# Top-k attention and two MLP layers: the second product in spare columns of a score bank, the mask from an unnegated threshold

## The chip, the cores and the metric

The kernel runs on one core of a Trainium2 chip. The metric is the device time of one execution, in microseconds (us); lower is better. Every comparison is between executions of whole kernels on the chip.

## The reference

```python
# q, k, v: (4, 8, 576, 64): batch, heads, sequence, head size
scores = scale * np.matmul(q, k.transpose(0, 1, 3, 2))       # scale = 1/8
kth = np.partition(scores, -32, axis=-1)[..., -32:-31]       # the 32nd largest of each row
scores = np.where(scores >= kth, scores, -1000000000.0)
attn = np.exp(scores - np.max(scores, axis=-1, keepdims=True))
attn = attn / (np.sum(attn, axis=-1, keepdims=True) + 1e-09)
x = np.matmul(attn, v)                                       # then laid out as 2304 tokens x 512
# two layers, weights 512 x 2048 and 2048 x 512 each
h = x @ w_in;  g = h * (1 / (1 + np.exp(-1.702 * h)));  x = g @ w_out
h = x @ w_in2; g = P3(h) / (1 + |b0| |h| + |b1| h*h + 1e-6);  out = g @ w_out2
# P3(h) = a0 + a1 h + a2 h*h + a3 h*h*h
```

## The kernel before

The 2304 tokens are cut into 18 tiles of 128. For each tile the attention goes through 8 heads, so there are 144 steps, numbered 0 to 143 and called heads here. The MLP layers work on groups of two tiles (one at the end), in units whose hidden rows fill one 128x512 block.

A head goes through these stations (lines of the kernel before):

- TensorE multiplies q and k into a score tile `S` (line 585), 128 rows by two halves of 288 columns. Each half lies in a PSUM bank of its own with room for 512. There are two `S` tiles, so four banks.
- VectorE finds the 32nd largest score of each row: four times the eight largest (`mx`, line 594), and between them three times those eight are struck out (`W`, line 596). The first pass reads `S`, the others `W`.
- VectorE negates the threshold (line 598). ScalarE subtracts it, and a Prelu with a slope of 2^100 sends what lies below it far down (line 599). With that `S` is read for the last time.
- VectorE makes the bias of the exponential (lines 600 and 601), ScalarE takes the exponential (line 602) and a 16-bit copy (line 604), GpSimd the rest that the copy leaves (line 606).
- A DMA transposes both into `AT` (one tile), and TensorE multiplies `AT` and `V` into a bank `misc` (line 625: 64 columns and one with the row sums).
- VectorE inverts the sums (line 635), and ScalarE scales the 64 columns into `x` (line 636).

The remaining PSUM banks are one for `misc`, which the small sums of line 310 use too, one for the hidden rows `h` of the MLPs (line 748), and two for their outputs `acc` (lines 830 and 833). `NH` and `NMISC` count the first two kinds. The MLPs' elementwise work is on ScalarE (lines 769, 784, 798, 799, 807), GpSimd (773, 809) and VectorE (777).

What each engine does and in which order is settled ahead of the run. Each operation carries a cost and a due time in heads, and a planner (`schedule`) puts it on its engine where it would be ready first. On the chip every engine then goes through its list in order. An operation that waits holds up all behind it on that engine. The due times of the second product and of what follows it come from `LAV`, in heads. `lock` tells the planner whether an operation keeps VectorE and GpSimd apart; it changes no instruction.

Of the kernel before, what the change touches and what calls it, by code (L numbers as in the profile page):

```python
# [19 lines left out]
FAR = 2.0 ** 100  # L20
# [188 lines left out]
def kernel(  # L209
# [69 lines left out]
    def misc():  # L279
        return buf("misc", [P, 512], F32, NMISC, pp)  # L280

# [9 lines left out]
    kc = cp.tile([P, 4], F32, name="kc")  # L291
    POOL.memset(kc[:, 2:3], scale)
    POOL.memset(kc[:, 3:4], -scale)
# [257 lines left out]
    def q_scale(t, hp, prio):  # L551

        qi = QI[t, hp // 2]
        ei = EI[t, hp] = buf("ei", [P, 2], F32, 3)

        def f():
            for r0, n, bb, _ in segs(t):
                r = slice(r0, r0 + n)
                POOL.tensor_scalar(ei[r], kc[r, 2:4], qi[r, 2:3], kinv[r, bb, hp:hp + 1], ALU.mult, ALU.mult)

        op("POOL", 2 * PTINY * len(segs(t)), f, [qi] + [KI[bb, hp] for _, _, bb, _ in segs(t)], [ei], prio)
# [10 lines left out]
    def attend(i, prio):  # L572
        t, h = divmod(i, H)
        qs, ei = QS[t, h // 4], EI[t, h // 2]
# [14 lines left out]
        nm = buf("nm", [P, 2], F32, 3)  # L589
# [25 lines left out]
    def attend_av(i, prio):  # L615
        t, h = divmod(i, H)
        sg = segs(t)
        at = ATS.pop(i)
        ps = misc()

        def av(r0, n, V):
            for j in range(KM + 1):
                kp = P if j < KM else ST + 1
                for x, lo, hi in ((0, D, 2 * D + 1), (0, 0, D), (1, D, 2 * D + 1)):
                    PE.matmul(ps[r0:r0 + n, :hi - lo], at[:kp, x, j, r0:r0 + n], V[:kp, h % 2, j, lo:hi],  # L625
                              start=(j == 0 and lo == D and x == 0), stop=(j == KM and x == 1), skip_group_check=True)

        if h == 0:
            XT[t] = buf("x", [P, DM], F32, NX)
        x = XT[t]  # L630
        for r0, n, bb, _ in sg:
            V = VS[bb, h // 2]
            op("PE", 0.5, lambda r0=r0, n=n, V=V: av(r0, n, V), [at] + [VS[b2, h // 2] for _, _, b2, _ in sg], [ps] + ([x] if h == 0 else []), prio)
# [273 lines left out]
    for t in range(NT):  # L907
        for hq in range(H // 4):
            at(t * H + 4 * hq - QLAG, q_prep, t, hq, t * H + 4 * hq - QLAG)
        for hp in range(H // 2):  # L910
            at(t * H + 2 * hp - 1, q_scale, t, hp, t * H + 2 * hp - 1)
    for i in range(NS):
        at(i, attend, i, i)
        at(i + LAV, attend_av, i, i)
# [3 lines left out]
    for layer, p0 in ((1, W1P), (2, W2P)):  # L918
        for f2 in range(NPAIR):
            at(p0 + f2 * WR, w_load, layer, f2, p0 + f2 * WR)  # L920
    for g, ts in enumerate(grans):
        p = max(first[max(gb[g])] - 3, W1P + NPAIR * WR)
        at(p, x_scale, g, p)
        for t in ts:
            at((t + 1) * H - 0.9 + LAV, x_done, t, (t + 1) * H - 0.9)
# [10 lines left out]
    for n, (layer, g, only) in enumerate(seq):  # L936
        done = only is None or only == len(grans[g]) - 1
        if layer == 1:
            p = max(p, (grans[g][-1 if only is None else only] + 1) * H + LAV + MLAG)
# [44 lines left out]
LAV = 1.5  # L984
NMISC = 1
NH = 1
# [23 lines left out]
FREE = ("t", "misc")  # L1010
# [30 lines left out]
```

## Time and profile before

| what | value |
|---|---|
| time, median of 3 runs | 1317.77 us (1316.63 to 1322.38) |
| the profiled execution's own time | 1319.38 us |
| its span in the profile | 1317.6 us |
| busy TensorE / VectorE / ScalarE / GpSimd | 80% / 82% / 80% / 67% of the span |

The span runs from the first to the last instruction that the profile shows; the execution's time has 1.8 us more around it. Busy shares are averages over stretches with different limits: from 0 to 400 us the weights of the MLPs are prepared beside the first heads, from 400 to 1110 us attention and MLPs run side by side, and behind that only MLP work is left.

### The profile page before, as it was taken

To read this page: it belongs to the slowest core of one execution; us is meant where nothing else is said; L and a number is where in the kernel's file an instruction comes from. 1 tells how busy PE (TensorE), PEld (TensorE's weight loads), DVE (VectorE), ACT (ScalarE), POOL (GpSimd) and SP (SyncE) were. 2 spreads that over 40 slices of the span, in tenths; PEclk is the share of its full clock that TensorE was granted. 3 is DMA by queue.
4 is the path that set the end of the run, shared out by engine and by line. 5 is a ranking of instruction groups with operands and counts; after the bars stand their busy time and mean duration, and the time that the engine had idled before them with its cause. 6 is when DMAs were issued, how large, how long until landed. Compare 5 with 4: busy or idle time off the path is not lost.

```text
span 1317.6 us, 25473 instructions
## 1 busy us (share of the span) xinstructions
PE 1058.3 (80%) x8812; PEld 711.5 (54%) x8812; DVE 1078.3 (82%) x2649; ACT 1050.6 (80%) x1939; POOL 881.1 (67%) x998
## 2 busy tenths in 40 slices
PE   1222474744699899999899999999999999999997
PEld 0111352523466566666656665665666577566664
DVE  4999999999999899999989999999999999202010
ACT  6767675767689988999999898888889889667674
POOL 5576774645556776888676688667767866656554
PEclk9999975875699999999989999999999999999999
DMA  9667789777747984797777469666856963734375
GB/s 268 166 186 199 195 240 261 219 213 144 148 67 155 207 187 81 164 216 161 164 196 189 77 162 207 142 131 160 184 112 142 219 116 83 182 118 147 119 237 187
DMA packets 366145, 222.40 MB, mean 169 GB/s; under 512 B 316608, under 2 KB 328896, under 8 KB 366016
## 3 DMA queue, kind: packets, MB, share of 16 engines
q1 hardware_dynamic: 366016, 220.78, 69.6%
q8 instruction: 69, 1.13, 0.4%
q14 instruction: 60, 0.49, 0.1%
HBM read 136.32 MB, written 13.11 MB: 113 GB/s over the span
## 4 chain that ended last, share of the span: by engine, by line
DVE 45%; PE 22%; ACT 13%; POOL 7%; DMA 6%; issue 6%; SPq 1%; POOLq 0%; ACTq 0%; DVEq 0%
DVE mx L594 15%; DVE W L596 13%; PE h L748 9%; PE acc L830 7%; ACT t L769 5%; DMA AT<-A 5%; PE acc L833 3%; POOL t L773 3%; DVE ring L357 3%; DVE ring L359 3%; DVE t L777 2%; POOL A L606 2%; DVE ring L355 2%; PE misc L625 1%; DVE V L462 1%
## 5 line engine op out<-in xcount | busy, mean ns | idle before, releaser
L773 POOL TENSOR_TENSOR t<-t,t 128x512 f32<-128x512 f32 x288 | 380.4, 1321 | 142.1 <-ACT t L769 72.8
L594 DVE MAX8 mx<-W 128x8 f32<-128x576 f32 x432 | 323.2, 753 | 5.2
L830 PE MATMUL acc<-ring,t 128*128 128x512 f32 x576 | 271.1, 603 | 7.3 <-POOL t L773 4.9
L606 POOL TENSOR_TENSOR A<-E,A 128x576 f16<-128x576 f32 x144 | 189.7, 1318 | 66.3 <-ACT A L604 57.0
L748 PE MATMUL h<-xh,W 128*128 128x128 f16 (+1 forms) x2304 | 214.8, 253 | 15.2 <-ACT t L769 13.4
L596 DVE MATCH_REPLACE8 W<-mx,W 128x576 f32<-128x576 f32 x288 | 213.5, 742 | 0.0
L748 PE MATMUL h<-yh,ring 128*128 128x256 f16 (+1 forms) x1920 | 201.8, 262 | 12.7 <-ACT t L769 12.2
L748 PEld LDWEIGHTS <-W 128*128 128x128 f16 x2304 | 186.6, 102 | 44.4 <-issue 24.0
L748 PEld LDWEIGHTS <-ring 128*128 128x128 f16 x1920 | 171.8, 98 | 57.0 <-issue 37.0
L585 PE MATMUL S<-K,qs 128*128 128x288 f16 (+1 forms) x640 | 118.6, 317 | 79.8 <-ACT E L599 74.6
L833 PE MATMUL acc<-W,gh 128*128 128x512 f16 x576 | 175.4, 387 | 2.4 <-ACT gh L807 2.4
L602 ACT ACTIVATE E<-E,nm,ei 128x576 f32<-128x576 f32 x144 | 124.3, 865 | 44.1 <-DVE nm L601 30.2
L777 DVE SCALAR_TENSOR_TENSOR t<-t,ab,t 128x512 f32<-128x512 f32 x72 | 65.3, 907 | 114.9 <-ACT t L769 114.7
L830 PEld LDWEIGHTS acc<-ring,t 128*128 128x128 f32 x576 | 102.1, 192 | 99.5 <-issue 89.2
L625 PEld LDWEIGHTS <-AT 128*128 128x128 f16 (+2 forms) x2400 | 96.3, 106 | 92.9 <-DMA AT<-A 66.3
L625 PE MATMUL misc<-V,AT 128*128 128x65 f16 (+5 forms) x2400 | 106.6, 202 | 47.6 <-DMA AT<-A 34.1
L599 ACT ACTIVATE E<-S,nm 128x576 f32<-128x576 f32 x144 | 106.4, 739 | 40.4 <-DVE nm L598 32.7
L769 ACT ACTIVATE t<-h,cf 128x512 f32<-128x512 f32 (+1 forms) x160 | 95.8, 638 | 39.9 <-PE h L748 31.2
L585 PEld LDWEIGHTS <-qs 128*128 128x128 f16 (+1 forms) x640 | 65.3, 110 | 111.0 <-issue 86.8
L594 DVE MAX8 mx<-S 128x8 f32<-128x576 f32 x144 | 108.6, 754 | 12.4 <-PE S L585 11.6
L809 POOL TENSOR_TENSOR gl<-t,gh 128x512 f16<-128x512 f32 x72 | 84.4, 1172 | 48.5 <-ACT gh L807 47.4
L833 PE MATMUL acc<-W,gl 128*128 128x512 f16 x288 | 111.2, 386 | 4.9 <-POOL gl L809 4.9
(145 smaller groups left out, 1729.5 us busy)
## 6 DMA issues: line engine op xcount, KB each, us to landing
ring<-scr SPq DMA_DIRECT2D x160, 512.0 KB, 3.9
ring<-in_moe_w_in_dram SPq DMA_DIRECT2D x16, 1024.0 KB, 5.7
ring<-in_moe_w_out_dram SPq DMA_DIRECT2D x16, 1024.0 KB, 6.0
ld<-in_v_dram SPq DMA_DIRECT2D x32, 256.0 KB, 3.4
out_dram<-t SPq DMA_DIRECT2D x18, 256.0 KB, 3.6
ld<-in_k_dram SPq DMA_DIRECT2D x16, 256.0 KB, 3.7
lq<-in_q_dram SPq DMA_DIRECT2D x32, 128.0 KB, 3.2
scr<-ring SPq DMA_DIRECT2D x8, 512.0 KB, 6.8
```

The costliest lines, as they stand in the source:

```text
L585: PE.matmul(s[:n, c, :SH], qs[:, 2 * (h % 4) + x, :n], K[:, h % 2, c * SH:(c + 1) * SH], start=(x == 0), stop=(x == 1))
L594: op("DVE", dve(S, not r), lambda r=r: DVE.max(mx[:, r], w.t if r else sv()), [w if r else s], [mx], prio)
L596: op("DVE", dve(S, not r) + 0.068, lambda r=r: DVE.match_replace(w.t if r else two(w.t), mx[:, r], w.t if r else sv(), NEG), [mx, w if r e ...
L599: op("ACT", act(S, True) + APA, lambda: ACT.activation(two(e.t), sv(), AF.Prelu, bias=nm[:, 0:1], alpha=FAR), [s, nm], [e], prio)
L602: op("ACT", act(S) + 2 * APA, lambda: ACT.activation(e.t, e.t, AF.Exp, bias=nm[:, 1:2], scale=ei[:, 0:1]), [e, nm, ei], [e], prio)
L606: lo = lambda en: en.tensor_tensor(A[:, 1, :S], e.t, A[:, 0, :S], ALU.subtract)
L625: PE.matmul(ps[r0:r0 + n, :hi - lo], at[:kp, x, j, r0:r0 + n], V[:kp, h % 2, j, lo:hi], start=(j == 0 and lo == D and x == 0), stop=(j == ...
L748: PE.matmul(o, w[:, half, kd * 256 + jj * P: kd * 256 + (jj + 1) * P], xy[:, tl, l * ND + kd, :], start=(n == 0), stop=(n == 3 * ND - 1))
L769: op("ACT", act(w, True) + APA, lambda f2=f2, c=c: ACT.activation(dst[:, c], src[:, c], func, bias=bias(f2) if bias else 0.0, scale=sc(f2) ...
L773: op("POOL", pool_tt(512), lambda: POOL.tensor_tensor(o.t, x.t, y.t, f), [x, y], [o], prio, alt=("DVE", dve(512), lambda: DVE.tensor_tenso ...
L830: PE.matmul(acc[j].t, u.gate[:, c], w[:, jj * DM:(jj + 1) * DM], start=st, stop=sp)
L833: PE.matmul(acc[j].t, l[:, c], w[:, half, jj * DM:(jj + 1) * DM], start=(st and n == 0), stop=(sp and n == 2))
```

## The change

```diff
-FAR = 2.0 ** 100
+NEAR = 2.0 ** -90
...
     def misc():
-        return buf("misc", [P, 512], F32, NMISC, pp)
+        return buf("h", [P, 512], F32, NH, pp)
...
 def q_scale(t, hq, prio):          # once per four heads; before, once per two
-                POOL.tensor_scalar(ei[r], kc[r, 2:4], qi[r, 2:3], kinv[r, bb, hp:hp + 1], ALU.mult, ALU.mult)
+                POOL.tensor_scalar(ei[r], kinv[r, bb, 2 * hq:2 * hq + 2], qi[r, 2:3], -scale / NEAR, ALU.mult, ALU.mult)
...
 def attend(i, prio):
+        if i >= LA:
+            av_product(i - LA, s, prio)
...
-        op("DVE", TINY, lambda: DVE.tensor_scalar(nm[:, 0:1], mx[:, 3, 7:8], -1.0, None, ALU.mult), [mx], [nm], prio)
-        op("ACT", act(S, True) + APA, lambda: ACT.activation(two(e.t), sv(), AF.Prelu, bias=nm[:, 0:1], alpha=FAR), [s, nm], [e], prio)
-        op("DVE", 2 * TINY, lambda: (DVE.tensor_scalar(nm[:, 1:2], mx[:, 3, 7:8], mx[:, 0, 0:1], ei[:, 0:1], ALU.subtract, ALU.mult),
-                                     DVE.tensor_scalar(nm[:, 1:2], nm[:, 1:2], EBITS * LN2, None, ALU.add)), [mx, ei], [nm], prio)
-        op("ACT", act(S) + 2 * APA, lambda: ACT.activation(e.t, e.t, AF.Exp, bias=nm[:, 1:2], scale=ei[:, 0:1]), [e, nm, ei], [e], prio)
+        op("ACT", act(S, True) + APA, lambda: ACT.activation(two(e.t), sv(), AF.Prelu, bias=mx[:, 3, 7:8], scale=-1.0, alpha=NEAR), [s, mx], [e], prio)
+        op("POOL", 2 * PTINY, lambda: (POOL.tensor_scalar(nm.t, mx[:, 0, 0:1], mx[:, 3, 7:8], es(), ALU.subtract, ALU.mult),
+                                       POOL.tensor_scalar(nm.t, nm.t, NEAR, EBITS * LN2, ALU.mult, ALU.add)), [mx, ei], [nm], prio, lock=False)
+        op("ACT", act(S) + 2 * APA, lambda: ACT.activation(e.t, e.t, AF.Exp, bias=nm.t, scale=es()), [e, nm, ei], [e], prio)
+        if i >= LA:
+            av_rows(i - LA, s, [e], prio)
...
-    def attend_av(i, prio):
-        ps = misc()
+    def av_product(i, s, prio):
...
-                    PE.matmul(ps[r0:r0 + n, :hi - lo], at[:kp, x, j, r0:r0 + n], V[:kp, h % 2, j, lo:hi],
+                    PE.matmul(s[r0:r0 + n, 0, SH:SH + hi - lo], at[:kp, x, j, r0:r0 + n], V[:kp, h % 2, j, lo:hi],
...
+    def av_rows(i, s, after, prio):
...
-        op("DVE", TINY, lambda: DVE.reciprocal(r.t, ps[:, D:D + 1]), [ps], [r], prio)
-        op("ACT", act(D, True) + APA, lambda: ACT.activation(x[:, h * D:(h + 1) * D], ps[:, :D], AF.Copy, scale=r.t), [ps, r], [x], prio,
-           alt=("DVE", dve(D, True) + APD, lambda: DVE.tensor_scalar(x[:, h * D:(h + 1) * D], ps[:, :D], r.t, None, ALU.mult)))
+        op("DVE", TINY, lambda: DVE.reciprocal(r.t, s[:, 0, SH + D:SH + D + 1]), [s, *after], [r], prio, lock=False)
+        op("DVE", dve(D, True) + APD, lambda: DVE.tensor_scalar(x[:, h * D:(h + 1) * D], s[:, 0, SH:SH + D], r.t, None, ALU.mult), [s, r, *after], [x], prio, lock=False)
...
-LAV = 1.5
-NMISC = 1
-NH = 1
+LA = 3
+NH = 2
```

The second product of head i - 3 is written into columns 288 to 352 of the first bank of the `S` tile of head i, ahead of that head's scores. Its rows are read only after the exponential of head i. The last three heads' second products come behind all scores in `S` tiles of their own. The bank that `misc` had goes to `h`, whose two banks the small sums now share. The Prelu takes the threshold itself as bias with a scale of -1 and a slope of 2^-90, and the scale of the exponential is negative and 2^90 times as large. The bias of the exponential moves from VectorE to GpSimd; the scaling of the 64 columns moves from ScalarE to VectorE.

VectorE's list around head 27, the first head whose scores it begins here (tile numbers behind the names; `r` is the inverted row sum of an earlier head). Before:

```order
L594 MAX mx_2676<-S_2655 128x8
L596 MATCH_REPLACE W_2679<-mx_2676,S_2655 128x576
L594 MAX mx_2700<-S_2671 128x8
L594 MAX mx_2676<-W_2679 128x8
L635 RECIPROCAL r_2708<-misc_2681 128x1
L596 MATCH_REPLACE W_2710<-mx_2700,S_2671 128x576
L596 MATCH_REPLACE W_2679<-mx_2676,W_2679 128x576
L594 MAX mx_2700<-W_2710 128x8
L594 MAX mx_2676<-W_2679 128x8
```

Of the change:

```order
L595 MAX mx_2763<-S_2739 128x8
L597 MATCH_REPLACE W_2772<-mx_2763,S_2739 128x576
L595 MAX mx_2763<-W_2772 128x8
L641 RECIPROCAL r_2777<-S_2695 128x1
L597 MATCH_REPLACE W_2772<-mx_2763,W_2772 128x576
L642 TENSOR_SCALAR x_2097<-S_2695,r_2777 128x64
L595 MAX mx_2763<-W_2772 128x8
L597 MATCH_REPLACE W_2772<-mx_2763,W_2772 128x576
L595 MAX mx_2763<-W_2772 128x8
```

Before, two heads (26 and 27) take turns, so that few rows stand directly behind the row of the same head whose result they use. Now head 27 stands alone, and the rows of line 641 and 642 are those of head 23, out of the `S` tile of head 26.

TensorE's list at head 86 (its scores, and the second product of head 83 out of `AT`; `h` and `acc` are MLP work). Before:

```order
L748 MATMUL h_8570<-xh_7408,W_82 128x256
L585 LDWEIGHTS qs_7888
L585 MATMUL S_8603<-K_7547,qs_7888 128x288
...
L625 LDWEIGHTS AT_8551
L625 MATMUL misc_8610<-V_6811,AT_8551 128x65
...
L830 MATMUL acc_1275_8016<-ring,t_8549 128x512
```

Of the change:

```order
L840 MATMUL acc_1184_7813<-ring,t_8177 128x512
L627 LDWEIGHTS AT_8326
L627 MATMUL S_8376<-V_6588,AT_8326 128x65
...
L586 LDWEIGHTS qs_7856
L586 MATMUL S_8376<-K_7331,qs_7856 128x288
...
L758 MATMUL h_8411<-xh_7409,W_80 128x256
```

The second product now stands ahead of the scores, in their tile, and both wait until that tile's earlier head has given up its rows.

## Rows read from the trace of the kernel before

**Rows 1.** The page, part 1: busy us (share of the span) and instructions of each engine.

```profile
PE 1058.3 (80%) x8812; PEld 711.5 (54%) x8812; DVE 1078.3 (82%) x2649; ACT 1050.6 (80%) x1939; POOL 881.1 (67%) x998
```

**Rows 2.** Windows by stage: us, busy of PE, PEld, DVE, ACT, POOL; clock, DMA.

```profile
0.00:400.00 400.00, 190.27 (x1691) 134.07 (x1692) 372.98 (x921) 278.87 (x527) 237.75 (x313) 0.84 0.74 192
400.00:1110.00 710.00, 673.82 (x5629) 451.71 (x5628) 664.06 (x1643) 632.85 (x1161) 524.47 (x582) 1.00 0.73 158
1110.00:1317.60 207.60, 194.24 (x1496) 125.75 (x1493) 41.29 (x87) 138.87 (x254) 118.88 (x104) 1.00 0.53 162
```

**Rows 3.** Windows of line 594 alone: four such instructions are one head.

```profile
0.00:400.00 400.00, 125.65 (x173) 0.84 0.74 192
400.00:1110.00 710.00, 295.44 (x396) 1.00 0.73 158
```

**Rows 4.** Waits from 400 to 1110 us: us in total, times, longest us.

```profile
ACT E L602 <- DVE nm L601: 21.7, 32, 2.0
...
PE misc L625 <- DMA AT<-A: 12.5, 17, 1.8
PE h L748 <- ACT t L769: 12.3, 15, 3.4
DVE r L635 <- PE misc L625: 11.8, 15, 3.8
...
DVE mx L594 <- PE S L585: 8.7, 16, 1.4
...
PE S L585 <- ACT E L599: 3.5, 4, 1.6
```

**Rows 5.** Groups by line and shape: busy us, mean ns of one.

```profile
L636 ACT ACTIVATE x<-misc,r 128x64 f32<-128x64 f32 x144 | 44.6, 310 | 31.3 <-DVE r L635 30.1 <-DVE nm L598 0.4
L559 POOL TENSOR_SCALAR ei<-kc,qi,kinv 128x2 f32<-128x2 f32 x64 | 30.3, 474 | 28.2 <-ACT E L602 27.2 <-POOL V L473 0.2
```

**Rows 6.** VectorE's timeline from 700 to 712 us: start, duration, instruction.

```profile
700.82 0.26 DVE L600 TENSOR_SCALAR nm<-mx,ei 128x1 f32<-128x1 f32 x1
701.11 0.15 DVE L601 TENSOR_SCALAR nm<-nm 128x1 f32<-128x1 f32 x1
701.19 0.08 DVE L596 MATCH_VALUE_LOAD W<-mx,W 128x8 f32 x1
...
702.03 0.76 DVE L594 MAX8 mx<-W 128x8 f32<-128x576 f32 x1
702.83 0.09 DVE L596 MATCH_VALUE_LOAD W<-mx,W 128x8 f32 x1
...
704.48 0.15 DVE L598 TENSOR_SCALAR nm<-mx 128x1 f32<-128x1 f32 x1
704.55 0.16 DVE L635 RECIPROCAL r<-misc 128x1 f32<-128x1 f32 x1
704.62 0.74 DVE L594 MAX8 mx<-S 128x8 f32<-128x576 f32 x1
705.28 0.79 DVE L777 SCALAR_TENSOR_TENSOR t<-t,ab,t 128x512 f32<-128x512 f32 x1
706.00 0.08 DVE L596 MATCH_VALUE_LOAD W<-mx,S 128x8 f32 x1
```

**Rows 7.** VectorE's timeline at 280 us.

```profile
280.02 0.75 DVE L594 MAX8 mx<-S 128x8 f32<-128x576 f32 x1
280.69 0.74 DVE L594 MAX8 mx<-W 128x8 f32<-128x576 f32 x1
```

**Rows 8.** Timeline of ScalarE and TensorE from 700 to 712 us.

```profile
700.06 0.73 ACT L599 ACTIVATE E<-S,nm 128x576 f32<-128x576 f32 x1
...
701.36 0.87 ACT L602 ACTIVATE E<-E,nm,ei 128x576 f32<-128x576 f32 x1
...
702.84 0.62 PE L625 MATMUL misc<-V,AT 128*128 128x65 f16 x15
...
703.30 0.65 PE L585 MATMUL S<-K,qs 128*128 128x288 f16 x4
```

More of the change, by code (lines that the diff above doesn't have):

```diff
@@ L290 @@
     b0, b1 = ab[:, 4:5], ab[:, 5:6]
-    kc = cp.tile([P, 4], F32, name="kc")
-    POOL.memset(kc[:, 2:3], scale)
-    POOL.memset(kc[:, 3:4], -scale)
+    kc = cp.tile([P, 1], F32, name="kc")
     POOL.memset(kc[:, 0:1], 1.0 + 1e-6)
@@ L549, in q_prep, with q_scale @@
         op("SP", 1.3, lambda: SP.dma_start_transpose(qs.t, qh.t.rearrange("p h x n -> p (h x n)")), [qh], [qs], prio, nbytes=P * DM * 5)
-    def q_scale(t, hp, prio):
-        qi = QI[t, hp // 2]
-        ei = EI[t, hp] = buf("ei", [P, 2], F32, 3)
+    def q_scale(t, hq, prio):
+        qi = QI[t, hq]
+        ei = EI[t, hq] = buf("ei", [P, 2], F32, 3)
         def f():
@@ L558, in f @@
                 r = slice(r0, r0 + n)
-                POOL.tensor_scalar(ei[r], kc[r, 2:4], qi[r, 2:3], kinv[r, bb, hp:hp + 1], ALU.mult, ALU.mult)
-        op("POOL", 2 * PTINY * len(segs(t)), f, [qi] + [KI[bb, hp] for _, _, bb, _ in segs(t)], [ei], prio)
+                POOL.tensor_scalar(ei[r], kinv[r, bb, 2 * hq:2 * hq + 2], qi[r, 2:3], -scale / NEAR, ALU.mult, ALU.mult)
+        op("POOL", PTINY * len(segs(t)), f, [qi] + [KI[bb, 2 * hq + x] for _, _, bb, _ in segs(t) for x in range(2)], [ei], prio)
     atiles = [cp.tile([P, 2, (KM + 1) * P], F16, name=f"A{j}") for j in range(NA)]
@@ L573, in attend @@
         t, h = divmod(i, H)
-        qs, ei = QS[t, h // 4], EI[t, h // 2]
+        qs, ei = QS[t, h // 4], EI[t, h // 4]
+        es = lambda: ei[:, h % 4 // 2:h % 4 // 2 + 1]
         sg = segs(t)
@@ L588, in attend @@
         mx = buf("mx", [P, 4, 8], F32, 3)
-        nm = buf("nm", [P, 2], F32, 3)
+        nm = buf("nm", [P, 1], F32, 3)
         w = buf("W", [P, S], F32, 2)
@@ L613 @@
     ATS = {}
-    def attend_av(i, prio):
+    def av_product(i, s, prio):
         t, h = divmod(i, H)
         sg = segs(t)
-        at = ATS.pop(i)
-        ps = misc()
+        at = ATS[i]
         def av(r0, n, V):
@@ L624, in av @@
                 for x, lo, hi in ((0, D, 2 * D + 1), (0, 0, D), (1, D, 2 * D + 1)):
-                    PE.matmul(ps[r0:r0 + n, :hi - lo], at[:kp, x, j, r0:r0 + n], V[:kp, h % 2, j, lo:hi],
+                    PE.matmul(s[r0:r0 + n, 0, SH:SH + hi - lo], at[:kp, x, j, r0:r0 + n], V[:kp, h % 2, j, lo:hi],
                               start=(j == 0 and lo == D and x == 0), stop=(j == KM and x == 1), skip_group_check=True)
+        for r0, n, bb, _ in sg:
+            V = VS[bb, h // 2]
+            op("PE", 0.5, lambda r0=r0, n=n, V=V: av(r0, n, V), [at] + [VS[b2, h // 2] for _, _, b2, _ in sg], [s], prio - 1)
+    def av_rows(i, s, after, prio):
+        t, h = divmod(i, H)
+        ATS.pop(i)
         if h == 0:
@@ L630, in attend_av @@
         x = XT[t]
-        for r0, n, bb, _ in sg:
-            V = VS[bb, h // 2]
-            op("PE", 0.5, lambda r0=r0, n=n, V=V: av(r0, n, V), [at] + [VS[b2, h // 2] for _, _, b2, _ in sg], [ps] + ([x] if h == 0 else []), prio)
         r = buf("r", [P, 1], F32, 3)
-        op("DVE", TINY, lambda: DVE.reciprocal(r.t, ps[:, D:D + 1]), [ps], [r], prio)
-        op("ACT", act(D, True) + APA, lambda: ACT.activation(x[:, h * D:(h + 1) * D], ps[:, :D], AF.Copy, scale=r.t), [ps, r], [x], prio,
-           alt=("DVE", dve(D, True) + APD, lambda: DVE.tensor_scalar(x[:, h * D:(h + 1) * D], ps[:, :D], r.t, None, ALU.mult)))
+        op("DVE", TINY, lambda: DVE.reciprocal(r.t, s[:, 0, SH + D:SH + D + 1]), [s, *after], [r], prio, lock=False)
+        op("DVE", dve(D, True) + APD, lambda: DVE.tensor_scalar(x[:, h * D:(h + 1) * D], s[:, 0, SH:SH + D], r.t, None, ALU.mult), [s, r, *after], [x], prio, lock=False)
+    def attend_av(i, prio):
+        s = buf("S", [P, 2, 512], F32, 2, pp)
+        av_product(i, s, prio)
+        av_rows(i, s, (), prio)
     grans, t = [], 0
@@ L909 @@
             at(t * H + 4 * hq - QLAG, q_prep, t, hq, t * H + 4 * hq - QLAG)
-        for hp in range(H // 2):
-            at(t * H + 2 * hp - 1, q_scale, t, hp, t * H + 2 * hp - 1)
+            at(t * H + 4 * hq - 1, q_scale, t, hq, t * H + 4 * hq - 1)
     for i in range(NS):
         at(i, attend, i, i)
-        at(i + LAV, attend_av, i, i)
     for layer in (1, 2):
@@ L920 @@
             at(p0 + f2 * WR, w_load, layer, f2, p0 + f2 * WR)
+    for i in range(NS - LA, NS):
+        at(NS + 0.1 * (i - NS + LA), attend_av, i, i)
     for g, ts in enumerate(grans):
@@ L924 @@
         for t in ts:
-            at((t + 1) * H - 0.9 + LAV, x_done, t, (t + 1) * H - 0.9)
+            at((t + 1) * H - 0.9 + LA, x_done, t, (t + 1) * H - 0.9)
     def first_layer(g):
@@ L938 @@
         if layer == 1:
-            p = max(p, (grans[g][-1 if only is None else only] + 1) * H + LAV + MLAG)
+            p = max(p, (grans[g][-1 if only is None else only] + 1) * H + LA + MLAG)
         for u in make_units(layer, g, only):
@@ L1009 @@
 PHASES = (16.0, 48.0, 130.0)
-FREE = ("t", "misc")
+FREE = ("t", "h")
 _INS = ['q', 'k', 'v', 'moe_w_in', 'moe_w_out', 'moe2_w_in', 'moe2_w_out', 'moe2_a', 'moe2_b']
```

## Prediction

> **What bounds the kernel now.** I read the stages first. Until 400 us VectorE is busy for 373 of 400 us and TensorE for 190 [rows 2]; 173 instructions of line 594 fall there, so some 43 heads, and 396, some 99 heads, up to 1110 us [rows 3]. In the second stage TensorE is busy for 674 of 710 us and VectorE for 664. Behind it VectorE has 41 us left, and TensorE is busy for 194 of 208 us. So the first stage is VectorE's, the last TensorE's, and in the middle both are nearly full. The page's 80% to 82% for three engines [rows 1] says nothing of this.
>
> Then the waits of the middle stage [rows 4]. TensorE's missing 36 us are mostly waits for the transposed `AT` (12.5 us), for ScalarE to empty the one bank `h` (12.3) and for `S` (3.5). VectorE waits 11.8 us for the second product, ahead of the inversion of its sums, and 8.7 us for scores.
>
> Last, VectorE's own spacing, since its rows overlap. From the start of one search for the largest to the start of the next, of another head, 0.67 us pass [rows 7]. Where the next instruction needs the first one's result it is 0.80 (702.03 to 702.83) [rows 6]: a dependent neighbour costs 0.13 us more, and anything that stands between the two fills that gap.
>
> **The change, part by part.**
>
> *VectorE, taken away.* By start-to-start times, line 600 holds the engine for 0.29 us, line 601 for 0.08, line 598 for 0.07 [rows 6], together 0.44 us a head; their durations add up to more (0.26 + 0.15 + 0.15), but overlap.
>
> *VectorE, added.* One scaling of 128x64 out of PSUM a head. No row shows it on this engine. From below: the inversion of one column holds it for 0.07 us (704.55 to 704.62). From above: the 512 columns of line 777 hold it for 0.72 (705.28 to 706.00) [rows 6], and ScalarE's own row for the same work lasts 0.31 [rows 5]. A line through 0.07 for 1 and 0.72 for 512 columns gives 0.15 for 64, which I take. By the section on the TRN2 errata of the Trainium skill's page "VectorE: DVE Perf Modes" such an operation out of PSUM takes 120 cycles and one for each element, an estimate of 0.19 us, which would make the first stage 1.6 us worse; no run here shows it yet.
>
> *VectorE, moved.* The order shows a loss. Of the six places in a head where a search and a strike-out of one head can stand directly behind each other, 14 in all do so in heads 0 to 43 before, and 89 after the change: the two heads that took turns now mostly come one after the other, because a score tile is given back later. In heads 44 to 143 it is 268 before and 244 after.
>
> So for heads 0 to 43, where VectorE sets the pace: 43 x 0.44 = 18.9 us less, 40 x 0.15 = 6.0 us more, (89 - 14) x 0.13 = 9.8 us more. That is 3 us gained. The bounds of the scaling make it 6 us gained (0.07) or 3 us lost (0.31). For the rest: 101 x 0.44 = 44 us less, and 28 places where line 598 stood directly behind its search, 3.6 us less; 104 x 0.15 = 15.6 us more; 24 x 0.13 = 3.1 us less. That is 35 us less for VectorE.
>
> On the gaps the Trainium skill's page "VectorE: DVE Perf Modes", section "The DRAIN you can't avoid", disagrees: it says that eight chained copies took the same time with a semaphore behind each and with one at the end, so that only the count matters. The trace's 0.80 against 0.67 speaks against that here. By the rule the first stage would gain 12.9 us in place of 3, and the whole would end 10 us lower.
>
> *TensorE, middle stage.* Its work stays the same: the same matrix products in other banks, and by the order almost the same MLP work between the same heads. With VectorE 35 us shorter, TensorE is the bound of this stage, and it can win back only what it waits: 36 us. The second product comes three heads behind instead of one and a half; at 710/99 = 7.2 us a head that is 11 us more for the transposition, against waits of at most 1.8 us [rows 4], so I take 10 of the 12.5 us. Two banks for `h` let one be filled while the other is read: 8 of the 12.3 us. New is that each head's second product and scores wait for the earlier head's inverted and scaled rows; TensorE has MLP products queued ahead of them, and when those are late, everything behind on its list is. I put 3 us on that, about what `S` costs now; bounds 0 and the last rival. Sum: 15 us.
>
> *The rest.* ScalarE loses 44.6 us [rows 5], and in the middle stage it was busy for 633 of 710 us: no bound, so nothing. GpSimd gets two one-column instructions a head; the nearest row, line 559 with its two pointers, takes 0.47 us [rows 5], so at most 0.95 us a head, 137 us, less half of line 559's calls, some 18 us. In the middle stage that is 525 + 94 - 12 = 607 us of about 695 us: full, but not the fullest. They have to be done while ScalarE runs the Prelu (0.73 us [rows 8]). If GpSimd is in the middle of another instruction, the exponential waits; it waits 21.7 us for line 601 now [rows 4]. I take these as equal, so nothing. The end stage: TensorE is idle for 13 us there, of which the second bank of `h` may take some; I leave that to the range. The DMAs are the same in number and size.
>
> **Sum.** The profiled execution took 1319.4 us (span 1317.6 and 1.8 around it), 1.6 us above the median of the runs. Less 3 and less 15 that is 1301 us, or 1300 by the median. I predict 1300 us, a gain of 1.4%. Its own range is 1286 to 1309 us: 14 us lower if all the waits of TensorE in the middle go, 9 higher if new ones take half of the gain.
>
> **The rivals.**
>
> *The waits go altogether.* VectorE gains the 13 us of the first stage because exposed gaps are filled by other work, TensorE wins back all of its 36 us in the middle and half of its 13 at the end: 1318 - 13 - 36 - 6 = 1263 us. For it: VectorE has 35 us of air in the middle. Against it: no stage shows TensorE busier than 95% so far (674 of 710 us, and 194 of 208 in the last [rows 2]). Half of it would be 1280.
>
> *GpSimd takes the wait over.* Its two instructions come behind other work more often than behind none, since it is busy for 525 of 710 us already [rows 2], and the exponential, then the inversion on VectorE (line 641, in order) and the scores behind that wait. 0.13 us for each of 144 heads eats the whole 18 us: no change, 1317 us. Against it: the planner puts these instructions in by their due time, ahead of the MLP's.
>
> *The score tile is given back too late: slower.* Now it is free behind the Prelu, after the change behind exponential, inversion and scaling. At 700 us: exponential ends at 702.23 [rows 8], the inversion goes in behind the next search at 702.83, the scaling one strike-out later at 703.7 and ends at 703.9; second product and scores take 0.62 + 0.65 us more [rows 8], to 705.2. The next head's search began at 704.62 [rows 6]. So here VectorE would stand still for 0.6 us, where the Prelu had been held up. At 0.27 us a head, 144 heads cost 39 us, and 1318 - 18 + 39 = 1339 us; it decides from 0.125 us a head upwards. Against it: in heads 44 to 143 the order has the inversion behind three or fewer of the next head's seven steps in 62 of 104 cases, and behind four in 35. At 0.8 us a step, three steps (2.4 us) are left behind the scaling where it is three, and two (1.6 us) where it is four, for 1.3 us of products, and VectorE has other work to put between.
>
> **How the numbers follow.** A measurement of this kernel can tell a change of about 0.5% from none, so faster is below 1311 us and slower above 1324. Chances: the forecast 0.44, the waits going to half or altogether (1263 to 1285) 0.24, GpSimd taking it over 0.14, the late score tile 0.18. The forecast's few cases above 1311 are within those 0.44 (0.03). Faster 0.66, within 0.5% 0.17, slower 0.17. The range for 8 in 10 reaches from 1270 us, which leaves out the lower part of the second case (0.06), to 1325 us, which leaves out most of the last (0.14).
>
> **What the profile would show.** Right: VectorE's busy time falls from 1078 to about 1020 to 1030 us, ScalarE's to 1006, GpSimd's rises to 960 to 1000; the first 43 heads end within 10 us of 400; no wait of TensorE for `AT`, fewer for `h`; in the middle TensorE at 97% and VectorE below it. Wrong: a wait of line 595 for the scores, or of line 641 for the exponential, of more than 20 us in all on VectorE, or first heads that end after 410 us (the tiles held too long); ScalarE's line 603 waiting for line 602 by more than 40 us (GpSimd); or TensorE at 98% and over with an end at 1270.

## The result, and the profile after

The changed kernel takes 1325.93 us, median of 6 runs (1323.8 to 1328.03), against 1318.44 us of the kernel before in the same runs: a ratio of 1.006 (95% interval 1.0045 to 1.0075). It is 0.6% slower. A gain of 1.4% was forecast.

First the page's part 1 of the changed kernel, which answers to [rows 1]:

```profile
PE 1051.2 (79%) x8812; PEld 710.4 (54%) x8812; DVE 1061.3 (80%) x2359; ACT 1024.1 (77%) x1797; POOL 959.7 (72%) x1244
```

Every engine but GpSimd is busy for less time than before, and yet the end comes later. The windows by stage, with the columns of [rows 2]:

```profile
0.00:400.00 400.00, 159.03 (x1440) 111.96 (x1441) 348.76 (x774) 250.54 (x448) 243.65 (x361) 0.83 0.73 187
400.00:1110.00 710.00, 683.75 (x5717) 461.01 (x5715) 657.94 (x1482) 623.09 (x1079) 584.11 (x765) 0.99 0.71 159
1110.00:1325.50 215.50, 208.38 (x1662) 137.38 (x1659) 54.60 (x105) 150.51 (x272) 131.89 (x119) 1.00 0.50 162
```

TensorE stands idle for 400 - 159.0 = 241.0 us in the first stage (209.7 before), for 26.2 in the middle (36.2) and for 7.1 at the end (13.4). That is 31.3 more, 10.0 less and 6.3 less, together 15 us more; its busy time is 7.1 us shorter, and the rest is the 7.9 us by which the span grew. So the middle and the end gained about as hoped, and the first stage lost twice as much. The searches alone (line 595, was 594) say the same in heads; they answer to [rows 3]:

```profile
0.00:400.00 400.00, 115.29 (x155) 0.83 0.73 187
400.00:1110.00 710.00, 304.10 (x408) 0.99 0.71 159
```

In the first stage 18 searches are missing, four and a half heads; in the middle there are 12 more. Next the waits of the changed kernel up to 400 us:

```profile
PE S L627 <- DVE x L642: 73.3, 18, 10.6
PEld L627 <- DMA AT<-A: 45.4, 13, 9.7
...
ACT E L603 <- POOL nm L602: 23.0, 12, 5.3
```

And VectorE's own up to 420 us:

```profile
DVE mx L595 <- PE S L586: 12.5, 10, 3.1
DVE ring L353 <- POOL W L381: 9.6, 3, 7.0
DVE p L307 <- POOL p L504: 8.4, 3, 7.8
DVE ring L353 <- DMA ring<-in_moe_w_in_dram: 3.9, 2, 2.3
DVE p L442 <- ACT lt L438: 3.9, 2, 3.5
DVE p L307 <- ACT yh L370: 3.3, 3, 2.0
DVE r L641 <- ACT E L600: 2.9, 2, 1.9
...
```

All such waits of VectorE up to 420 us add up to 50.2 us, and to 24.4 in the kernel before. VectorE set the pace of this stage with few gaps; now it stands still for 26 us more, 10 of them for scores, most of the rest for weights whose preparation runs through all engines. The long waits of TensorE are the place to look at. Its timeline, then VectorE's and ScalarE's, of the changed kernel from 266 to 287 us (start, duration, instruction; the idle time before it and its releaser in brackets):

```profile
266.59 0.97 PE L627 MATMUL S<-V,AT 128*128 128x65 f16 x15 [2.20 <-DVE x L642]
267.38 1.15 PE L586 MATMUL S<-K,qs 128*128 128x288 f16 x4
274.48 0.97 PE L627 MATMUL S<-V,AT 128*128 128x65 f16 x15 [5.96 <-DVE x L642]
275.27 1.15 PE L586 MATMUL S<-K,qs 128*128 128x288 f16 x4
276.21 8.21 PE L758 MATMUL h<-xh,W 128*128 128x128 f16 x120
284.69 0.64 PE L627 MATMUL S<-V,AT 128*128 128x65 f16 x15 [0.27 <-DMA AT<-A]
285.16 0.65 PE L586 MATMUL S<-K,qs 128*128 128x288 f16 x4
```

```profile
273.21 0.15 DVE L641 RECIPROCAL r<-S 128x1 f32<-128x1 f32 x1
...
274.06 0.27 DVE L642 TENSOR_SCALAR x<-S,r 128x64 f32<-128x64 f32 x1
274.26 0.75 DVE L595 MAX8 mx<-W 128x8 f32<-128x576 f32 x1
...
276.46 0.77 DVE L595 MAX8 mx<-S 128x8 f32<-128x576 f32 x1 [1.40 <-PE S L586]
...
281.49 0.76 DVE L595 MAX8 mx<-W 128x8 f32<-128x576 f32 x1
283.28 0.17 DVE L641 RECIPROCAL r<-S 128x1 f32<-128x1 f32 x1 [1.03 <-ACT E L600]
283.49 0.28 DVE L642 TENSOR_SCALAR x<-S,r 128x64 f32<-128x64 f32 x1
285.92 0.77 DVE L595 MAX8 mx<-S 128x8 f32<-128x576 f32 x1 [2.15 <-PE S L586]
```

```profile
268.86 0.74 ACT L600 ACTIVATE E<-S,mx 128x576 f32<-128x576 f32 x1 [0.22 <-DVE mx L595]
272.32 0.87 ACT L603 ACTIVATE E<-E,nm,ei 128x576 f32<-128x576 f32 x1 [2.72 <-POOL nm L602]
```

The Prelu has read its score tile by 269.60. Before the change the next scores could go in then. Now the tile also holds an earlier head's second product, and the rows that read it stand further down VectorE's list: the scaling begins at 274.06. TensorE waits 5.96 us, does product and scores in 1.94 us (274.48 to 276.42), and VectorE has run dry at 275.06. Behind those scores TensorE has 120 MLP products on its list; they now begin late, at 276.21, and the next scores wait behind them until 285.16. VectorE runs dry again, for 1.03 and 2.15 us. The exponential does not hold the tile: at 283.28 the inversion goes ahead while the exponential is still to come. The plan alone puts these rows behind it; on the chip they wait for the Prelu and for what stands ahead of them on VectorE's list.

The middle stage, with the columns of [rows 4]:

```profile
DVE mx L595 <- PE S L586: 28.4, 31, 3.2
...
ACT E L603 <- POOL nm L602: 11.4, 16, 1.3
...
PE S L627 <- DVE x L642: 8.2, 8, 1.5
...
PE S L627 <- DMA AT<-A: 5.0, 6, 2.0
```

TensorE's waits for `AT` fell from 12.5 to 5.0 us, those for the one `h` bank (12.3) to 1.3, and 8.2 us for scaled rows are new. VectorE waits longer for scores (8.7 before), which TensorE, now the fuller of the two, delivers when it can.

### The profile page after: what moved, and what is told of

Read it like the earlier page. It is cut to its first block, busy times and chain, and to the rows that moved or that the text cites. A ratio compares the mean times of both kernels' runs of the same rounds, so it can differ in the third digit from the quotient of the medians.

```text
span 1325.5 us, 25426 instructions
## 1 busy us (share of the span) xinstructions
PE 1051.2 (79%) x8812; PEld 710.4 (54%) x8812; DVE 1061.3 (80%) x2359; ACT 1024.1 (77%) x1797; POOL 959.7 (72%) x1244
## 4 chain that ended last, share of the span: by engine, by line
PE 39%; DVE 21%; POOL 16%; ACT 14%; issue 5%; DMA 5%; SPq 0%; POOLq 0%; DVEq 0%; ACTq 0%
PE h L758 16%; PE acc L843 9%; PE acc L840 8%; DVE mx L595 6%; DVE W L597 6%; POOL t L783 5%; ACT t L779 5%; PE S L586 3%; PE S L627 3%; POOL A L609 3%; DMA AT<-A 2%; DVE ring L355 2%; DVE ring L357 2%; POOL nm L601 2%; ACT A L607 1%
## 5 line engine op out<-in xcount | busy, mean ns | idle before, releaser
L783 POOL TENSOR_TENSOR t<-t,t 128x512 f32<-128x512 f32 x288 | 379.0, 1317 | 111.0 <-ACT t L779 50.2
L840 PE MATMUL acc<-ring,t 128*128 128x512 f32 x576 | 268.5, 606 | 12.5 <-POOL t L783 12.5
L609 POOL TENSOR_TENSOR A<-E,A 128x576 f16<-128x576 f32 x144 | 193.5, 1344 | 51.5 <-ACT A L607 49.5
L627 PE MATMUL S<-V,AT 128*128 128x65 f16 (+5 forms) x2400 | 107.6, 203 | 139.2 <-DVE x L642 81.6
L758 PE MATMUL h<-xh,W 128*128 128x128 f16 (+1 forms) x2304 | 208.8, 250 | 2.8 <-DMA xh<-xs 1.4
L758 PEld LDWEIGHTS <-W 128*128 128x128 f16 x2304 | 183.6, 100 | 32.9 <-issue 10.1
L600 ACT ACTIVATE E<-S,mx 128x576 f32<-128x576 f32 x144 | 106.5, 740 | 62.3 <-DVE mx L595 42.7
L586 PE MATMUL S<-K,qs 128*128 128x288 f16 (+1 forms) x640 | 121.7, 322 | 17.9 <-ACT E L600 10.4
L779 ACT ACTIVATE t<-h,cf,cf 128x512 f32<-128x512 f32 (+1 forms) x160 | 111.8, 738 | 0.0
L601 POOL TENSOR_SCALAR nm<-mx,ei 128x1 f32<-128x1 f32 x144 | 78.2, 543 | 46.3 <-DVE mx L595 29.5
```

The lines of the kernel that those rows point to most:

```text
L609: lo = lambda en: en.tensor_tensor(A[:, 1, :S], e.t, A[:, 0, :S], ALU.subtract)
L627: PE.matmul(s[r0:r0 + n, 0, SH:SH + hi - lo], at[:kp, x, j, r0:r0 + n], V[:kp, h % 2, j, lo:hi], start=(j == 0 and lo == D and x == 0), st ...
L758: PE.matmul(o, w[:, half, kd * 256 + jj * P: kd * 256 + (jj + 1) * P], xy[:, tl, l * ND + kd, :], start=(n == 0), stop=(n == 3 * ND - 1))
L779: op("ACT", act(w, True) + APA, lambda f2=f2, c=c: ACT.activation(dst[:, c], src[:, c], func, bias=bias(f2) if bias else 0.0, scale=sc(f2) ...
L783: op("POOL", pool_tt(512), lambda: POOL.tensor_tensor(o.t, x.t, y.t, f), [x, y], [o], prio, alt=("DVE", dve(512), lambda: DVE.tensor_tenso ...
L840: PE.matmul(acc[j].t, u.gate[:, c], w[:, jj * DM:(jj + 1) * DM], start=st, stop=sp)
```

## The experiments

The theory after the result: **the held tile**. A score tile that is kept past the Prelu for an earlier head's rows, with that product ahead of the scores on TensorE's list, takes away the cover under which VectorE worked in the first stage. The rival: **GpSimd**, whose two small operations a head delay the exponential (23.0 us of waits in the first stage) and whatever runs beside them. A second rival, that **any new plan** moves the time by as much, has a control. The kernel before takes 1318 to 1320 us in all of these runs. For each kernel the start of a head's first search (the one that reads `S`) in the profiled execution tells the stage:

```
kernel           time us  ratio (95%)               head 24   head 32   head 40   head 48   head 143
before                                                278.2     327.0     379.4     429.6     1116.7
after            1325.93  1.0060 (1.0045 to 1.0075)   303.1     353.1     410.0     463.6     1124.4
bank_only        1347.68  1.0222 (1.0200 to 1.0243)   305.0     358.1     420.1     477.6     1159.6
mask_only        1323.24  1.0035 (1.0018 to 1.0053)   287.7     334.9     384.5     441.0     1123.7
rows_early       1321.19  1.0026 (1.0010 to 1.0041)   294.7     346.9     404.9     458.1     1120.4
late_switch      1304.58  0.9896 (0.9882 to 0.9911)   281.0     329.9     379.9     453.9     1100.3
hold_back        1319.97  1.0016 (1.0000 to 1.0032)   291.8     343.7     396.5     461.0     1117.5
switch_32        1301.50  0.9876 (0.9854 to 0.9899)   282.4     332.2     395.6     453.8     1101.6
never_tile       1314.76  0.9979 (0.9966 to 0.9992)   280.3     329.7     379.3     438.6     1115.7
nudge_a          1317.91  1.0000 (0.9982 to 1.0017)   279.2     328.3     379.8     430.3     1118.0
bias_dve         1316.05  0.9984 (0.9966 to 1.0002)   280.1     330.9     379.8     449.0     1111.2
bias_early       1307.95  0.9904 (0.9871 to 0.9937)   280.2     330.4     379.3     448.6     1106.2
switch_ld3       1307.78  0.9901 (0.9868 to 0.9934)   282.0     334.7     383.2     457.6     1105.4
switch_two_at    1292.92  0.9799 (0.9769 to 0.9830)   285.7     334.3     382.5     434.9     1094.8
two_at           1324.55  1.0042 (1.0025 to 1.0060)   298.0     354.9     408.7     465.4     1120.8
before_two_at    1315.77  0.9986 (0.9968 to 1.0005)   281.2     330.5     381.5     434.5     1110.9
two_at_32        1311.34  0.9934 (0.9913 to 0.9954)   285.3     334.0     388.3     448.2     1108.3
```

**The halves alone.** bank_only is the changed kernel with the mask as before:

```diff
-        op("ACT", act(S, True) + APA, lambda: ACT.activation(two(e.t), sv(), AF.Prelu, bias=mx[:, 3, 7:8], scale=-1.0, alpha=NEAR), [s, mx], [e], prio)
+        op("DVE", TINY, lambda: DVE.tensor_scalar(nm[:, 0:1], mx[:, 3, 7:8], -1.0, None, ALU.mult), [mx], [nm], prio)
+        op("ACT", act(S, True) + APA, lambda: ACT.activation(two(e.t), sv(), AF.Prelu, bias=nm[:, 0:1], alpha=FAR), [s, nm], [e], prio)
...
```

> The change without its mask part: the product goes into the score tile and h has two banks, but threshold and bias are made on VectorE as before. Held-tile theory (the score tile is given back too late, so that the first 40 heads no longer take turns): at most 158 searches by 400 us, as in the change (156; before 173), and 1322 to 1345 us, since VectorE has 0.44 us a head more. GpSimd theory (the exponential and the weights' preparation wait behind the two bias instructions on GpSimd): 168 searches or more by 400 us and below 1312 us.

mask_only is the kernel before with that part of the change alone, the same lines the other way round.

> The kernel before with the mask part alone: threshold as bias, exponential's bias on GpSimd, product in its own bank and scaled on ScalarE as before. Held-tile theory: 172 searches or more by 400 us, and 1298 to 1318 us, since VectorE loses 0.44 us a head and nothing is held longer. GpSimd theory: at most 162 searches by 400 us and 1322 us or more.

Measured: 1347.68 and 1323.24 us. The bank half alone reaches head 40 at 420.1 us, 41 us late, and makes up nothing behind it (739.5 us from head 40 to head 143, 737.3 before); its time lies 3 us above the range of the held-tile theory, its 151 searches within it. The mask half alone has head 40 at 384.5: it takes small operations off VectorE, and the first stage loses 5 us. Its 171 searches by 400 us lie near the held-tile theory, its time is GpSimd's, so it fits neither. The loss of the first stage is mostly the bank half's, and each half alone is slower; the mask half is worth some 22 us where the bank half is (bank_only against the changed kernel), 10 of them up to head 40.

**When the tile is let go.** rows_early plans the rows behind the Prelu, not behind the exponential:

```diff
         op("ACT", act(S, True) + APA, lambda: ACT.activation(two(e.t), sv(), AF.Prelu, bias=mx[:, 3, 7:8], scale=-1.0, alpha=NEAR), [s, mx], [e], prio)
+        if i >= LA:
+            av_rows(i - LA, s, [e], prio)
...
-        if i >= LA:
-            av_rows(i - LA, s, [e], prio)
```

> The change with the inverted and scaled rows waiting for the Prelu only, not for the exponential (about 0.9 us less of holding the tile, and no wait for GpSimd in it). Held-tile theory: 160 to 168 searches by 400 us and 1308 to 1320 us. GpSimd theory by way of VectorE's wait for the exponential: the same. GpSimd theory by way of the weights' preparation: no difference, 154 to 158 and 1324 to 1328 us.

Measured: 1321.19 us, head 40 at 404.9, 157 searches by 400 us, between the theories. Earlier rows give back 5 of the 30 us.

late_switch gives the products of heads 0 to 39 a bank of `h` of their own, one and a half heads behind, and uses the score tiles from head 40 on:

```diff
 def attend_av(i, prio):
+        if i < LS:
+            s = buf("h", [P, 1, 512], F32, NH, pp)
+            av_product(i, s, prio, 0)
+            av_rows(i, s, (), prio, 0)
+            return
...
-        if i >= LA:
+        if i >= LS + LA:
...
+LS = 40
```

> The change from head 40 on only: the products of heads 0 to 39 go into an h bank 1.5 heads later, as before into misc, and their score tiles are free behind the Prelu; mask part and the rest as in the change. Held-tile theory: 170 searches or more by 400 us, the middle stage's gain of some 25 us kept, 1292 to 1306 us. GpSimd theory: at most 160 by 400 us and 1318 us or more.

Measured: 1304.58 us, head 40 at 379.9: the whole loss is gone, with GpSimd's part in place. never_tile is the same with `LS = 144`, so no product in a score tile at all.

> late_switch with no product in a score tile at all: all of them in the two h banks, mask part and scaling on VectorE as in the change. If the middle stage's gain is due to the product's own place and its 1.5 heads more (TensorE not waiting for the transposed tile): middle as before, 730 to 740 us from head 40 to 143, and 1315 to 1325 us. If two banks for h and VectorE's relief are enough: 712 to 722 us and 1295 to 1305 us.

Measured: 1314.76 us. Head 40 comes at 379.3, much as in late_switch, so 30 us are the price of the score tile in the first stage (410.0 in the changed kernel). But from head 40 to head 143 it needs 736.4 us, as the kernel before, where late_switch needs 720.4. Its waits in the middle stage show why:

```profile
PE h L627 <- DMA AT<-A: 17.2, 13, 3.2
DVE r L641 <- PE h L627: 16.4, 14, 3.4
```

With products one and a half heads behind in banks shared with the MLPs these waits are no shorter than before the change [rows 4]. Later products in the score tiles are what the middle stage gains from. hold_back tries the tile's holding alone. It is late_switch, and for heads 0 to 39 VectorE inverts one column of the scores behind the exponential (the result is not used), which keeps the tile that long with no product in it:

```diff
+        if i < LS:
+            hold = buf("hold", [P, 1], F32, 3)
+            op("DVE", TINY, lambda: DVE.reciprocal(hold.t, s[:, 0, 0:1]), [s, e], [hold], prio, lock=False)
```

> late_switch with one more thing for heads 0 to 39: behind the exponential VectorE inverts one column of the head's score tile into a tile that nobody reads, so that the tile is held as long as in the change, with no product in it. Held-tile theory: at most 162 searches by 400 us (late_switch 171) and 1318 to 1335 us. If it was not the holding but the product's place in front of the scores: 168 or more and 1303 to 1310 us (40 x 0.15 us more on VectorE at most).

Measured: 1319.97 us, head 40 at 396.5, 17 us behind late_switch, nearly all of which stays to the end (15.4 us). Holding alone is thus about half of the 30 us. The other half comes with the product in the tile: ahead of the scores on TensorE's list, and three heads behind in place of one and a half; no run takes these apart.

VectorE's idle time up to the start of head 40 (that time less its busy time in it) shows where the loss lies: 26.9 us in the kernel before, 29.2 in late_switch, 42.4 in hold_back and 52.7 in the changed kernel. Its busy time is 352.5, 350.7, 354.1 and 357.3 us. The planner's orders go the same way: dependent neighbours in heads 0 to 43 number 14, 39, 57 and 89.

These windows count the searches up to 400 us, of bank_only, late_switch and hold_back in this order:

```profile
0.00:400.00 400.00, 111.92 (x151) 0.84 0.73 186
```
```profile
0.00:400.00 400.00, 125.66 (x171) 0.84 0.76 192
```
```profile
0.00:400.00 400.00, 120.16 (x163) 0.83 0.74 189
```

**A new plan by itself.** nudge_a is the kernel before with one due time moved, which orders the same instructions anew:

```diff
-OLAG = 2.51
+OLAG = 2.53
```

> The kernel before with one due time changed (the MLP's second product 2.53 heads behind the first, not 2.51), so that the planner writes another order with the same instructions. It shows what a new order by itself moves: if the change's 7 us are no more than that, this differs from before by 5 us or more either way; else by less than 3 us.

Measured: 1317.91 us, a ratio of 1.0000. One other order moved nothing; it is one order, of the kernel before.

**GpSimd's part.** bias_dve is late_switch with the two operations of the exponential's bias on VectorE for all heads, bias_early for heads 0 to 39:

```diff
+        be = DVE if i < BV else POOL
-        op("POOL", 2 * PTINY, lambda: (POOL.tensor_scalar(nm.t, mx[:, 0, 0:1], mx[:, 3, 7:8], es(), ALU.subtract, ALU.mult),
+        op("DVE" if i < BV else "POOL", 2 * (TINY if i < BV else PTINY), lambda: (be.tensor_scalar(nm.t, mx[:, 0, 0:1], mx[:, 3, 7:8], es(), ALU.subtract, ALU.mult),
...
+BV = 144
```

> late_switch (1304.6 us) with the exponential's two small bias operations on VectorE for all heads, as before; the rest of the mask part, the late switch and the score bank from head 40 stay. Theory 'the held tile alone': where the bias is worked out is worth little, since 19 us of VectorE's work taken away gave nothing before; the time lies within 8 us of late_switch (1297 to 1312), with 168 to 174 searches by 400 us. Rival 'GpSimd's bias costs': the exponential's waits for it (23.0 us in the first 400 us of after) and the lengthened preparation of weights go, and the time falls below 1296. Rival 'VectorE sets the first stage': its 19 us come back there, under 165 searches by 400 us and over 1315.

> late_switch with the bias on VectorE for heads 0 to 39 alone, on GpSimd from head 40. Theory 'the held tile alone': within 6 us of late_switch, 168 to 174 searches by 400 us. Rival 'GpSimd's small operations slow VectorE's preparation of weights in the first stage' (the third ring operation took 1627 ns beside them, 1408 ns before): it takes some 32 times 0.2 = 6 us less, the first heads gain, and the time lies at 1290 to 1299. Rival 'VectorE sets the first stage': over 1312.

Measured: 1316.05 and 1307.95 us. In the first stage it makes no difference (head 40 at 379.8 and 379.3, and at 379.9 in late_switch). The three operations on `ring` that prepare the weights, here of late_switch and then of bias_early up to 400 us, do take less time with the bias on VectorE, 113.0 us together against 122.5, but VectorE has the bias to work out in return.

```profile
L357 DVE SCALAR_TENSOR_TENSOR ring<-ring 128x1024 int32<-128x1024 int32 x32 | 49.9, 1559 | 0.1
...
L355 DVE SCALAR_TENSOR_TENSOR ring<-ring 128x1024 int32<-128x1024 int32 x32 | 42.9, 1340 | 0.1
...
L353 DVE TENSOR_SCALAR ring<-ring 128x1024 int32<-128x1024 int32 x32 | 29.7, 934 | 5.9 <-DMA ring<-in_moe_w_in_dram 3.8 <-POOL W L381 2.0
```
```profile
L355 DVE SCALAR_TENSOR_TENSOR ring<-ring 128x1024 int32<-128x1024 int32 x32 | 44.2, 1382 | 0.1
L357 DVE SCALAR_TENSOR_TENSOR ring<-ring 128x1024 int32<-128x1024 int32 x32 | 42.5, 1329 | 0.1
...
L353 DVE TENSOR_SCALAR ring<-ring 128x1024 int32<-128x1024 int32 x32 | 26.3, 827 | 8.5 <-DMA ring<-in_moe_w_in_dram 5.2 <-POOL W L381 3.2
```

Behind head 40 it does: bias_dve is 8 us slower than bias_early, and 4.5 us of that show between head 40 and head 143 of the profiled executions. bias_early itself spreads from 1302 to 1315 us, and takes 6.5 us more than late_switch over those heads, where both have the same operations; differences of this size can be the order's. The time of bias_dve is the one that the rival on VectorE gave, but not its place, for 172 searches fall before 400 us; the windows of the middle stage, of bias_dve and then of bias_early, show VectorE at 682 of 710 us against 652:

```profile
400.00:1110.00 710.00, 674.02 (x5678) 453.77 (x5677) 681.97 (x1657) 614.93 (x1063) 511.61 (x553) 1.00 0.72 158
```
```profile
400.00:1110.00 710.00, 677.54 (x5709) 458.63 (x5708) 652.25 (x1465) 618.67 (x1069) 579.67 (x757) 0.99 0.73 159
```

**Where it is switched.** switch_32 has `LS = 32`.

> late_switch with the products in the score tile from head 32 on. In late_switch heads 40 to 47 took 70 us (before 50), with three products in a row ahead of the scores of head 43. If that queue of transpositions is what costs there: heads 40 to 47 in 50 to 56 us, and 1286 to 1298 us in all. If the switch costs wherever it stands: 1301 to 1310 us.

Measured: 1301.50 us. Wherever the switch stands, the eight heads behind it take long: 63 us for heads 32 to 39 here, 74 us for heads 40 to 47 in late_switch (70 in the expectation, 4 too few), where the kernel before takes 52 and 50. At the switch in late_switch the products of heads 38, 39 and 40 come one behind the other on TensorE's list, with MLP work but no scores between them, and each needs the one `AT` tile. Two such tiles find room only with three load tiles (for the weights' raw rows) in place of four. So switch_ld3 is the control, and switch_two_at has both:

```diff
-NLD = 4
+NLD = 3
...
-NAT = 1
+NAT = 2
```

> late_switch with three load tiles for W's raw rows in place of four, which is what makes room for switch_two_at; a control. Both theories: within 6 us of late_switch (1299 to 1311), heads 40 to 47 again some 70 us.

> switch_ld3 with two tiles for the transposed exponential in place of one, so that a transposition need not wait for the product before it. Theory 'at the switch three products and their transpositions queue behind one tile': heads 40 to 47 fall from 70 us to 50 to 58, TensorE's waits for AT in the middle (13 us in late_switch) to under 5, and the time to 8 to 20 us under switch_ld3. Rival 'the queue stands on scores and rows, not on AT': heads 40 to 47 stay at 65 to 70 us and the time within 6 us of switch_ld3.

Measured: 1307.78 and 1292.92 us. The queue is gone: heads 40 to 47 take 52.4 us, 74.4 in the control. The scores between 384 and 416 us (line 586) tell it, in switch_ld3 and then in switch_two_at; four such instructions are one head here:

```profile
L586 PE MATMUL S<-K,qs x8: 286/286/286, 385.8 to 394.3; 128*128 128x288 f16 x8
```
```profile
L586 PE MATMUL S<-K,qs x17: 283/286/297, 388.3 to 416.0; 128*128 128x288 f16 x17
```

In the control no score is computed from 394.3 us to the end of this stretch, though TensorE is busy with MLP work; with two tiles they come every 5 to 10 us. TensorE's waits for `AT` in the middle stage fall from 15.5 to 3.9 us.

Is that the change's gain, or the second tile's alone? two_at is the changed kernel, before_two_at the kernel before, each with the same two numbers.

> The changed kernel (score bank from head 0) with two tiles for the transposed exponential and three load tiles. Theory 'TensorE's queue behind rows and the held score tile make the first stage long': a second AT tile takes away the waits of the product for AT (45 us in the first 400 us of after) but not the 73 us in which the product waits for the rows of two heads before; head 40 still starts at 400 us or later, and the time is 1305 to 1322, at least 12 us above switch_two_at (1292.9). Rival 'the one AT tile was the whole loss': head 40 starts at 380 to 385 us and the time is 1290 to 1298, as switch_two_at.

> The kernel before with two tiles for the transposed exponential and three load tiles, nothing of the change. Theory 'in the steady stage the change takes away waits of its own (for the h banks and for row sums on ScalarE)': the second tile alone brings the kernel before to 1303 to 1316, at least 10 us above switch_two_at. Rival 'all that switch_two_at gains is the second tile': 1290 to 1298.

Measured: 1324.55 and 1315.77 us. The second tile alone gives neither kernel anything that can be told. The changed kernel stays 3 us above the range of the theory, with head 40 still at 408.7. With the second tile, the change with score tiles from head 40 on (its mask part and its two `h` banks included) is worth 1315.8 - 1292.9 = 23 us, and score tiles in the first 40 heads cost 26 at head 40 (408.7 against 382.5) and 32 at the end. two_at_32 moves the switch of switch_two_at to head 32:

> switch_two_at with the switch at head 32 in place of 40. Theory: with the queue at the switch gone, where it stands matters little as long as the first stage's heads don't hold their score tiles; heads 32 to 39 take under 55 us, and the time is 1288 to 1298. Rival 'any head of the first stage that holds its tile costs 0.75 us': eight such heads, 6 us more, 1298 to 1304.

Measured: 1311.34 us, a miss for both: 18 us more, where switch_32 was 3 us faster than late_switch. Heads 32 to 39 take 54.3 us against 48.2 in switch_two_at, 6 us more, which is the rival's 0.75 us a head. But heads 40 to 47 take 7.5 us more as well (59.9 against 52.4), though they hold their tiles in both kernels; the remaining 4 to 5 us of the 18 do not show between the profiled executions (1311.66 and 1297.37 us). The order has 39 dependent neighbours in heads 0 to 43 against 23 in switch_two_at, which points to the held tile again. Where the other 12 us come from stays open.

## Why the prediction was wrong

**The step that failed** is the first stage, the term "VectorE, moved" and the sum around it, which took VectorE's time as its work plus 0.13 us for each dependent neighbour and left its idle time as it was: 3 us gained were forecast, 31 us are lost at head 40. Of these 31, 26 are idle time of VectorE (52.7 us against 26.9) and 5 are busy time. Three things were wrong in the step.

- It let every microsecond taken off VectorE count there. mask_only against before shows that the 17.6 us of VectorE's small operations in the first 40 heads (0.44 us a head) are worth nothing in this stage as long as two heads take turns, and late_switch against bias_early shows it of the bias alone. In mask_only VectorE is busy up to head 40 for only 3 us less than before (349.4 against 352.5): the three operations on `ring` take 9 us longer (123.1 against 114.4), and 23 more dependent neighbours (37 against 14 in heads 0 to 43) are another 3 us by the forecast's price. Its idle time grew by 8 us.
- It priced the lost alternation at 0.13 us for each dependent neighbour, 9.8 us. But the two heads that took turns also were the cover: while one waited, the other kept VectorE busy. With one head at a time every late score, and every late weight, is a gap.
- The rival "the score tile is given back too late" was priced with rows at 700 us, for all heads alike. It was right as a mechanism, and the signs named for it came (first heads that end after 410 us). Its place was wrong. The middle stage, from which its rows came, gained on balance with the products in the tiles (720.4 us of late_switch against 736.4 of never_tile, head 40 to head 143). In the first stage the tile stays held for 4.5 us behind the Prelu in the stretch above, and product and scores take 0.97 and 1.15 us there where the rows at 700 us had 0.62 and 0.65. The granted clock is at the lower level of 1.2 GHz in this stretch, behind long idle times of TensorE, and back at 2.4 GHz after the 120 products:

```profile
262.00:276.00 14.00, 4.04 (x40) 3.03 (x41) 12.92 (x38) 9.89 (x14) 9.11 (x18) 0.50 0.67 168
...
284.00:290.00 6.00, 5.73 (x71) 4.03 (x69) 3.94 (x7) 5.86 (x13) 4.54 (x5) 1.00 1.35 298
```

The clock is hardly a part of the difference, though: over the whole stage the granted share is 0.83, and 0.84 before, and at 276 us the kernel before takes 1.03 and 1.15 us for the same two.

30 us over 40 heads are 0.75 us a head, against a deciding 0.125 over all 144.

That the whole came out only 7.5 us slower is the sum of two misses: the first stage lost 31 us, and behind it more was won back than the forecast had.

**The middle stage** held in kind: 15 us were forecast, and 10 us less idle time of TensorE were measured there, 6 more at the end stage, which had been left to the range. Counted by heads it is more: heads 40 to 143 take 714.4 us, 737.3 before, 23 us less, since TensorE's busy time behind head 40, taken as unchanged, also fell by some 7 us. Of the parts, the waits for `AT` gave 7.5 of the 10 us, the second `h` bank 11 where 8 were taken, and the waits for scaled rows cost 8.2 where 3 were taken.

**The scaling** was taken at 0.15 us. From its start to the start of the next instruction it holds VectorE for 0.19 us, the median of all 144 (0.20 in the stretch above, 274.06 to 274.26). The estimate of 0.19 us from the errata section of the Trainium skill's "VectorE: DVE Perf Modes" is borne out by this trace. Against 0.15 us that makes 2 us in the first stage and 6 in all.

**GpSimd** was taken as nothing. In the first stage that is right as a sum; its waits there (23.0 us) hide, since the exponential does not hold the tile. In the middle stage the exponential's waits for the bias halved (21.7 to 11.4 us), and the move of the bias is worth some 8 us (bias_dve against bias_early, one pair of orders), which the forecast had only as air on VectorE. GpSimd's busy time came out as forecast (960). VectorE's did not: 1061 against 1020 to 1030 us. ScalarE's is 1024 against 1006.

One sum of the prediction is loose, with no weight on the outcome: half of the first rival's 55 us would end at 1290 us; 1280 lies half-way from the forecast.

## What to carry to other kernels

A resource that is kept longer must be priced in every stage in which it is used, with that stage's own rows: here the same tile paid for itself where TensorE is full, and cost 30 us where one engine sets the pace and two heads taking turns are all the cover it has. So look at what alternates before the change and doesn't after it, and count the lost cover, not only the lost pipelining. And if a change gains in one stage and loses in another, switch it on where it gains, and see what queues up at the switch: switch_two_at does both and is 2.0% faster than the kernel before.

## What was unexpected of the hardware

VectorE's three integer operations on 128x1024 of the weights, 32 times each, do not always take the same time. With the exponential's bias on VectorE they take 113.0 us together in bias_early and 114.4 in the kernel before, with it on GpSimd 122.5 in late_switch and 123.1 in mask_only. But with it on GpSimd they also take 114.1 in rows_early and 115.2 in hold_back, and with it on VectorE 117.4 in bank_only. So GpSimd's one-column work beside them does not explain it by itself; the cause stays open.

A GpSimd operation on one column with two per-row operands (line 601) takes 376 ns in the median and up to 2.4 us, where VectorE took 0.26 us [rows 6]. The row of the changed kernel by line (minimum, median and maximum in ns, first and last start):

```profile
L601 POOL TENSOR_SCALAR nm<-mx,ei x144: 357/376/2396, 47.6 to 1134.3; 128x1 f32<-128x1 f32 x144
```

Not tried: the second product behind the scores in the same tile, which would free the scores from waiting for `AT`.
